# Attention on one core: scores, maxima and sums of the loop share eight PSUM banks by a build-time reckoning, half of the maxima 512 wide

## The chip, the core and the metric

The kernel runs on one core of a Trainium2 chip. The metric is device time in microseconds (us) from start to end of one execution. The core's engines run beside each other and wait for each other by semaphores: TensorE (PE in the profile; its weight loads are the row PEld), VectorE (DVE), ScalarE (ACT), GpSimd (POOL) and SyncE (SP), which here issues the DMAs. PE writes its results to PSUM, which has eight banks of 512 float32 values in each of 128 partitions; DVE and ACT read them there.

## What is computed

Two attention layers, A and B, are computed from inputs of 2048 rows of 640 columns, with 32 heads of 20 columns each. A looks back over 8 positions with a step of 2; B is full attention, and B is what the loop below does. The two results stand side by side in the output.

```python
# A: per head, 8 keys and values at distance 0, 2, .. 14
logits = jnp.where(mask, jnp.einsum("bhsd,bhswd->bhsw", q, kg) * Dh**-0.5, -1e9)
o_a = jnp.einsum("bhsw,bhswd->bhsd", softmax(logits), vg)   # then @ wo
# B: per head, all 2048 keys
scores = jnp.einsum("bhqd,bhkd->bhqk", q, k) * Dh**-0.5
o_b = jnp.einsum("bhqk,bhkd->bhqd", softmax(scores), v)     # then @ wo
```

## The kernel before

Before the loop PE projects A's and B's inputs to queries, keys and values. A's attention itself is done by POOL, in pieces that are handed out along the program; A's output projection is 32 pieces (`a_out`) of 15 matmuls of 320 columns each, and these pieces are worked into B's loop. They are called fills below.

B's loop (lines 794 to 838) runs over 512 steps. Heads are taken in 8 groups of 4, queries in 4 chunks of 512, keys in 16 blocks of 128: a step is one block of keys for one chunk of queries and one group. In step i:

- `b_qk` (644) makes the scores of four heads, keys in partitions and queries in columns: two planes (`pl`) of two matmuls (`r`). Each matmul uses 62 rows, and the two of a plane stand in the upper and the lower half of PE's rows, so that they run side by side. ACT takes the exponential of each into a tile e, 512 wide.
- `b_pv` (666) multiplies the exponentials of step i - 2 (LAG) with the values, in 8 PE passes; the row of ones among the values gives the sums. Two steps are added up in one bank, and ACT copies it out in every second step.
- `b_max` (618) finds the row maxima that step i + 24 (LEAD) will need. Scores are made once more, with queries in partitions, four matmuls of 512 columns; DVE takes the maximum of two banks in one instruction (1024 wide), twice a step. Maxima are turned, split and brought by DMA into the query tile (`max_rows`, 559), so that the score matmul itself subtracts them.

PSUM is shared in a fixed way: four single banks (`bank`, `give`, lines 87 to 99), used in turn by scores, sums and fills, and two double banks (`wide`, 101) for maxima. The order on every engine is the order in which the program calls the operations: `InOrder` (47) keeps it. In a step it is: first plane of scores, values of step i - 2, second plane of scores, first maximum, then perhaps a fill (every third pair of steps at most, lines 834 to 837), second maximum. Other work is due at a given step: `after(n, fn)` puts it n steps on, `tick` runs what is due, and `odd` moves some of it to steps of one parity.

In the last 24 steps no maxima are left; there scores use the double banks too. This tail (line 811) is followed by B's last output projection.

Of the kernel before, what the change touches and what calls it, by code (L numbers as in the profile page):

```python
# [2 lines left out]

# [5 lines left out]
F32 = mybir.dt.float32  # L9
F32R = mybir.dt.float32r  # L10
AF = mybir.ActivationFunctionType
ALU = mybir.AluOpType
# [20 lines left out]
BS = 3 * DH  # L33
# [13 lines left out]
class InOrder:  # L47


    def __init__(self, tc, engine):  # L50
        self.tc, self.engine = tc, engine

    def __getattr__(self, name):
        op = getattr(self.engine, name)
        return lambda *a, **k: self.tc.keep_in_program_order(op(*a, **k))  # L55


@with_exitstack
def attention_pair(ctx, tc, xa, wqk_a, wv_a, wo_a, xb, wqk_b, wv_b, wo_b, oa, ob):
# [3 lines left out]
    sb = ctx.enter_context(tc.tile_pool(name="sb", bufs=1))  # L63
    ps = ctx.enter_context(tc.tile_pool(name="ps", bufs=1, space=PS))
    dr = ctx.enter_context(tc.tile_pool(name="dr", bufs=1, space=bass.MemoryType.DRAM))
    pe, dve, act, gp, sp = (InOrder(tc, e) for e in (nc.tensor, nc.vector, nc.scalar, nc.gpsimd, nc.sync))


    now = [0]
# [14 lines left out]
            fn(*args)  # L84


    free = list(range(4))
    taken = {}

    def bank():  # L90

        n = free.pop(0)
        t = ps.tile([128, 512], F32, tag=f"st{n}", bufs=1, name="ps_st")
        taken[id(t)] = (n, t)
        return t

    def give(t):

        free.append(taken.pop(id(t))[0])

    def wide():

        return ps.tile([128, 2, 512], F32, tag="mx", bufs=2, name="ps_mx")

    def all_banks():
        while True:
# [452 lines left out]
    def max_rows(m4, m1, q, qc):  # L559

        mt = sb.tile([128, 3, 32], F32R, tag="mtr", bufs=2, name="mtr")
        md = dr.tile([2, GH * 512], F32, tag="mdr", bufs=4, name="mdr")
        raw = mt[:, 0].bitcast(F32)

        def turn():

            dve.transpose(raw, m1)

        def parts():
            gp.tensor_copy(mt[:, 1], raw)  # L570
            gp.tensor_tensor(mt[:, 2], raw, mt[:, 1].bitcast(F32), ALU.subtract)

        def store():
            for b in range(4):
                sp.dma_start(md.rearrange("t (j b c) -> b j t c", b=4, c=32)[b], mt[32 * b:32 * b + 16, 1:].bitcast(F32))

        def load():
            for r in range(2):
                sp.dma_start(q[r * HALF + BS:r * HALF + BM, qc].bitcast(F32),
                             md[:, r * 1024:(r + 1) * 1024].rearrange("t (p c) -> t p c", p=2))  # L580
        t = odd(1)
        after(t, dve.tensor_reduce, m1[:, :16], m4.rearrange("p r a c -> p (r a) c"), AX.X, ALU.max)
        after(t, turn)
        after(t + 1, parts)
        after(t + 3, store)
        after(t + 4, load)
# [28 lines left out]
    for t in m1s:  # L615
        gp.memset(t, 0.0)

    def b_max(i):

        u, sub = divmod(i, NKB)  # L620
        g, qc = divmod(u, NQC)
        q, k, v = stacks[g]
        if sub == 0:
            mxt[u] = (sb.tile([128, 2, 8, 4], F32, tag="mx4", bufs=2, name="mx4"),
                      m1s[u % 2])
        m4, m1 = mxt[u]
        pq, ch = divmod(sub, 2)
        pl, qb = divmod(pq, 4)
        for c in (2 * ch, 2 * ch + 1):
            p = wide()  # L630
            for r in range(2):
                rows = slice(r * HALF, r * HALF + BS)
                pe.matmul(p[:, r], q[rows, qc, pl, qb * 128:qb * 128 + 128],
                          k[rows, pl, c * 512:(c + 1) * 512], start=True, stop=True)
            dve.tensor_reduce(m4[:, :, pq, c], p, AX.X, ALU.max)
            if c % 2 == 0:
                yield
        if sub == NKB - 1:
            max_rows(m4, m1, q, qc)

    P = {}
    accs, raws, spare = {}, {}, []

    def b_qk(i):
        u, kb = divmod(i, NKB)
        g, qc = divmod(u, NQC)
        q, k, v = stacks[g]
        P[i] = []
        for pl in range(2):
            w = wide() if pl and i + LEAD >= NS else None  # L650
            ps2 = [bank() for _ in range(2)] if w is None else [w[:, 0], w[:, 1]]
            for r in range(2):
                rows = slice(r * HALF, r * HALF + BM)
                pe.matmul(ps2[r], k[rows, pl, kb * 128:kb * 128 + 128], q[rows, qc, pl], start=True, stop=True)
            if i + LEAD >= NS and i % 2:
                e = sb.tile([128, 2, 512], F32, tag="akv", bufs=4, name="e")
            else:
                e = sb.tile([128, 2, 512], F32, tag="p", bufs=PB, name="e")
            for r in range(2):
                act.activation(e[:, r], ps2[r], AF.Exp, scale=SCALE)  # L660
                if w is None:
                    give(ps2[r])
            P[i].append(e)
            yield

    def b_pv(i):
        u, kb = divmod(i, NKB)
        g, qc = divmod(u, NQC)
        n, part = divmod(kb, 2)
        if part == 0:  # L670
            accs[u] = bank()
        acc = accs[u]
        for j in range(GH):
            pe.matmul(acc[32 * j:32 * j + 32, :], stacks[g][2][:, kb, j * VC:j * VC + 32], P[i][j % 2][:, j // 2],
                      start=(part == 0), stop=(part == 1))
        del P[i]
        if part == 0:
            return
        if n == 0:
            raws[u] = sb.tile([128, 512], F32, tag="raw", bufs=2, name="braw")  # L680
            act.copy(raws[u], acc)
        else:
            more = spare[n % 2][:, n // 2 % 2]
            act.copy(more, acc)
            after(1, pool, raws[u], raws[u], more, ALU.add)
        give(accs.pop(u))
        if kb == NKB - 1:
            last = g == NG - 1
            normalize(raws.pop(u), g, qc * 512, 2 if last else 5, (lambda: out_last(qc)) if last else None)


    outs_b = {}
# [53 lines left out]
    for n, half, s in V_GROUPS[:-LAG]:  # L746
        v_group(n, half, s)
        tick()
        groups += 1
        if q_loads:  # L750
            for _ in range(4):
                q_loads.pop(0)()
        if groups == 1:
            wait[0] = 5
        if groups in (8, 16):
            XB[groups // 8 - 1], more = x_pieces(xb, groups // 8 - 1, gp)
            for fn in more:
                fn()
        if groups > 6:
            for i in islice(steps, 1):  # L760
                for _ in b_max(i):
                    pass
        if groups > 16 and groups % 3 == 0 and groups != 21:
            next(a_work, None)
        if groups in (26, 28):
            v_piece(0, *((0, 4) if groups == 26 else (8, 16)))
# [5 lines left out]
    def load_out(src, W, halves=range(2)):  # L772
        for h in halves:
            w, more = wide_pieces(src[h], gp)
            W.append(w)
            loads.extend(more)
# [14 lines left out]

    WO_b = []
    loop[0] = now[0] + 1
    for i in range(NS + LAG):
        g, sub = divmod(i, NQC * NKB)
        if sub == 4 and g + 1 < NG:
            k_loads, q_loads = b_pieces(g + 1)
            for n, fn in enumerate(k_loads + q_loads + [lambda g=g + 1: v_piece(g, 0, NKB)]):
                after(1 + 2 * n, fn)
        if i in (NS - 56, NS - 40):  # L800
            out_first((i - NS + 56) // NKB)
        tick()
        if loads and i % 2:
            loads.pop(0)()
        if i % 14 in (1, 5, 7, 11) and next(a_work, 0) == 0:
            for d in done_a:
                d[0] -= 1
        if done_a and done_a[0][0] <= 0:
            a_turn(*done_a.pop(0)[1:])
        turn_parts()  # L810
        if i + LEAD >= NS:

            for _ in b_qk(i) if i < NS else ():
                pass
            if i % 2:
                b_pv(i - LAG - 1)
                b_pv(i - LAG)
                if fill:
                    fill.pop(0)()
            continue  # L820
        qk = b_qk(i) if i < NS else iter(())
        next(qk, None)
        if i >= LAG:
            b_pv(i - LAG)
        else:
            v_group(*v_late.pop(0))
            if not v_late:
                load_out(wo_a, WO, (1,))

                spare += [sb.tile([128, 2, 512], F32, tag="last0", bufs=2, name="more") for _ in range(2)]  # L830
        next(qk, None)
        mx = b_max(i + LEAD)
        next(mx, None)
        if fill and i % 2 == 0:
            fill.pop(0)()
        elif i % 6 == 4 and not out_piece() and not left_a[0] and not WO_b:
            load_out(wo_b, WO_b)
        next(mx, None)


    qc = NQC - 1
# [54 lines left out]
```

## Time and profile before

| | us |
|---|---|
| median of 3 runs | 1843.13 |
| lowest and highest run | 1841.50 and 1843.66 |
| the profiled execution | 1841.84 |
| its span, first to last instruction | 1840.0 |
| PE busy in the span | 1796.4 |
| ACT busy | 1356.7 |
| DVE busy | 1318.5 |
| POOL busy | 1214.9 |

The granted clock of PE is 0.999 over the span. Names are those of the program's tiles: ps_st is a single bank, ps_mx a double one, e the exponentials, mx the maxima, bq and bk B's queries and keys, vb its values, ww and aot the output weights and A's turned result, more and braw the sums copied out. "out<-in" is what an instruction writes and reads. All instructions bear line L55, that of the helper that records them, so rows are told apart by engine and tiles. A row of the order of time has start, length, engine, operation and count, and in square brackets how long the engine stood idle before it and what ended that. A row of the waits has who waited for whom, the total in us, how often, and the longest.

### The profile page before, as it was taken

To read this page: it belongs to the slowest core of one execution; us is meant where nothing else is said; L and a number is where in the kernel's file an instruction comes from. 1 tells how busy PE (TensorE), PEld (TensorE's weight loads), DVE (VectorE), ACT (ScalarE), POOL (GpSimd) and SP (SyncE) were. 2 spreads that over 40 slices of the span, in tenths; PEclk is the share of its full clock that TensorE was granted. 3 is DMA by queue.
4 is the path that set the end of the run, shared out by engine and by line. 5 is a ranking of instruction groups with operands and counts; after the bars stand their busy time and mean duration, and the time that the engine had idled before them with its cause. 6 is when DMAs were issued, how large, how long until landed. Compare 5 with 4: busy or idle time off the path is not lost. (4 is left out here: it accounts for less than half of the span.)

```text
span 1840.0 us, 30597 instructions
## 1 busy us (share of the span) xinstructions
PE 1796.4 (98%) x11211; PEld 961.8 (52%) x11211; DVE 1318.5 (72%) x1350; ACT 1356.7 (74%) x2597; POOL 1214.9 (66%) x1072
## 2 busy tenths in 40 slices
PE   9999999999999999999999999999999999999999
PEld 8888888886344343343343333433434434433568
DVE  3100332278898989989989999899898898899400
ACT  4222322224898989989989999899898898899891
POOL 0000076028999999989999999999999872254232
PEclk9999999999999999999999999999999999999999
DMA  6323686656543544354435435344544331121023
GB/s 224 111 93 107 206 297 243 214 175 181 149 131 114 142 140 124 112 149 139 122 98 143 152 112 152 111 137 120 152 144 115 93 101 55 36 71 49 28 69 112
DMA packets 193006, 240.23 MB, mean 131 GB/s; under 512 B 90972, under 2 KB 121308, under 8 KB 191864
## 3 DMA queue, kind: packets, MB, share of 16 engines
q1 hardware_dynamic: 192280, 237.63, 42.4%
q8 instruction: 88, 1.44, 0.3%
q10 hardware_dynamic: 576, 0.66, 0.1%
q14 instruction: 62, 0.51, 0.1%
HBM read 173.29 MB, written 64.91 MB: 129 GB/s over the span
## 5 line engine op out<-in xcount | busy, mean ns | idle before, releaser
L55 DVE TENSOR_REDUCE mx<-ps_mx 128x2 f32<-128x1024 f32 x1024 | 1198.3, 1217 | 133.8 <-PE ps_mx L55 131.9
L55 ACT ACTIVATE e<-ps_st 128x512 f32<-128x512 f32 x2000 | 1063.4, 608 | 50.3 <-PE ps_st L55 22.2
L55 PE MATMUL ps_st<-e,vb 128*32 128x512 f32 x4096 | 543.6, 605 | 0.6
L55 PE MATMUL ps_st<-bq,bk 62*128 62x512 f32 x2000 | 471.0, 455 | 2.0 <-DMA bq<-mdr 2.0
L55 PEld LDWEIGHTS ps_st<-bq,bk 62*128 62x128 f32 x2000 | 249.4, 184 | 424.4 <-ACT e L55 408.2
L55 PE MATMUL ps_mx<-bk,bq 60*128 60x512 f32 x2048 | 421.0, 442 | 34.9 <-DVE mx L55 16.7
L55 POOL TENSOR_TENSOR braw<-braw,more 128x512 f32<-128x512 f32 x224 | 287.7, 1284 | 178.5 <-ACT more L55 170.4
L55 POOL TENSOR_TENSOR akv<-akv,aq 128x1280 f32<-128x1280 f32 x64 | 188.9, 2952 | 237.4 <-DMA akv<-ka_d 237.4
L55 PEld LDWEIGHTS ps_mx<-bk,bq 60*128 60x128 f32 x2048 | 192.1, 185 | 203.5 <-DVE mx L55 193.5
L55 POOL TENSOR_TENSOR akv<-akv 128x640 f32<-128x640 f32 (+3 forms) x304 | 281.4, 926 | 23.8
L55 PEld LDWEIGHTS ps_st<-e,vb 128*32 128x32 f32 x4096 | 82.0, 108 | 157.2 <-ACT e L55 82.0
L55 ACT COPY ro<-ps_st 128x320 f32<-128x320 f32 (+1 forms) x92 | 43.6, 474 | 154.7 <-PE ps_st L55 110.1
L55 POOL TENSOR_TENSOR akv<-akv,al 128x1280 f32<-128x1280 f32 x64 | 151.5, 2367 | 0.2
L55 ACT COPY more<-ps_st 128x512 f32<-128x512 f32 x224 | 132.8, 593 | 12.9 <-PE ps_st L55 2.8
L55 PE MATMUL ps_st<-ww,xn 128*128 128x320 f32 x720 | 120.1, 315 | 0.0
L55 PEld LDWEIGHTS ps_st<-ww,xn 128*128 128x128 f32 x720 | 106.6, 188 | 20.9 <-ACT e L55 9.1
L55 POOL TENSOR_TENSOR xn<-stg,xn 128x512 fp32r<-128x512 f32 (+1 forms) x20 | 30.1, 1508 | 94.8 <-ACT xn L55 93.5
L55 DVE TENSOR_TENSOR wc<-stg,wc 128x480 fp32r<-128x480 f32 (+5 forms) x15 | 8.4, 559 | 101.5 <-ACT wc L55 101.5
L55 PE MATMUL ps_st<-ww,aot 128*128 128x320 f32 x480 | 79.0, 316 | 0.0
L55 POOL TENSOR_TENSOR ao<-ao,akv 128x640 f32<-128x640 f32 x48 | 74.9, 1560 | 3.8
L55 DVE TENSOR_TENSOR xl<-stg,xl 128x512 fp32r<-128x512 f32 x12 | 8.3, 689 | 96.2 <-ACT xl L55 96.2
L55 PEld LDWEIGHTS ps_st<-ww,aot 128*128 128x128 f32 x480 | 70.5, 188 | 11.7 <-ACT e L55 5.8
(84 smaller groups left out, 1312.2 us busy)
## 6 DMA issues: line engine op xcount, KB each, us to landing
akv<-ka_d SPq DMA_DIRECT2D x128, 320.0 KB
akv<-va_d SPq DMA_DIRECT2D x128, 320.0 KB
kb_d<-pr SPq DMA_DIRECT2D x20, 512.0 KB
qb_d<-pr SPq DMA_DIRECT2D x20, 512.0 KB
bk<-kb_d SPq DMA_DIRECT2D x16, 640.0 KB
bq<-qb_d SPq DMA_DIRECT2D x64, 160.0 KB
rb<-s_d SPq DMA_DIRECT2D x128, 64.0 KB
stg<-xb SPq DMA_DIRECT2D x12, 512.0 KB
```

The costliest lines, as they stand in the source:

```text
L55: return lambda *a, **k: self.tc.keep_in_program_order(op(*a, **k))
```

## The change

All of PSUM becomes one tile of eight banks, psb. Before the loop and in its tail, banks are given out as before: 0 to 3 singly, 4 to 7 in two doubles.

In the steps with maxima the loop goes by pairs of steps (`b_pair`). The 8 score matmuls and 8 maximum matmuls of a pair are put in eight brackets of two (`b_two`), one matmul in each half of PE's rows. Four brackets hold a score and one matmul of a maximum; two hold both matmuls of a maximum, two hold two scores. A maximum whose matmuls share a bracket is reduced 1024 wide from two banks in a row, the others 512 wide, one bank each: per pair two wide and four narrow instead of four wide.

Which bank each matmul writes is chosen while the program is built. `InOrder` adds up a time for ACT and DVE with each operation, `b_pv` and `b_two` do so for PE, and `read_at` holds for each bank when its last reader should be done. `one` picks the bank that is ready first, `two` the two neighbours. The program that results is fixed; the waits in it still follow the real data. A fill takes a bank by the same reckoning, and is issued in odd steps, behind the fifth bracket of a pair (its second `yield`). Work that is due at odd steps now falls behind the third bracket. The diff's core:

```diff
+        def emit(*a, **k):
+            self.us += self.fixed + max([math.prod(x.shape[1:]) for x in a if hasattr(x, "shape")], default=0) / self.rate
+            return self.tc.keep_in_program_order(op(*a, **k))
...
+    dve, act = InOrder(tc, nc.vector, 0.075, 960), InOrder(tc, nc.scalar, 0.111, 1400)
...
+    psb = ps.tile([128, 8, 512], F32, name="ps_st")
...
     def bank():
 
+        if read_at:
+            n = one(pe.us)
+            pe.us = max(pe.us, read_at[n]) + 2.2
+            act.us = max(act.us, pe.us + 0.05)
+        else:
+            n = free.pop(0)
+        t = psb[:, n]
...
+    def one(t, *but):
+
+        at = [1e9] + read_at + [1e9]
+        return min((n for n in range(8) if n not in but), key=lambda n: (
+            max(t, read_at[n]), -max(t, at[n]) - max(t, at[n + 2])))
+
+    def two(t):
+
+        return min(range(7), key=lambda n: (max(t, read_at[n], read_at[n + 1]), abs(read_at[n] - read_at[n + 1])))
...
     def b_pv(i):
...
+        if read_at:
+            t = max(pe.us + 0.12, exp_at.pop(i))
+            if part == 0:
+                o = one(t)
+                accs[u] = o, psb[:, o]
+                t = max(t, read_at[o])
+                read_at[o] = 1e9
+            pe.us = t + 0.866
+            behind_v[0] = True
...
+    def b_two(what):
+
+        t = pe.us + 0.129 * behind_v[0]
+        lag = 0.53 if behind_v[0] else 0.44
+        both = what[0][0] == what[1][0] == "m"
+        if both:
+            n = two(t)
+            ns, ts = (n, n + 1), [max(t, read_at[n], read_at[n + 1])] * 2
+        else:
+            ns, ts = [], []
+            for _ in range(2):
+                ns.append(one(max([t] + ts), *ns))
+                ts.append(max([t] + ts + [read_at[ns[-1]]]))
+        pe.us = ts[1] + (0.236 if ts[1] > ts[0] + 0.05 or (ts[0] < t + 0.02 and not behind_v[0]) else 0.336)
+        behind_v[0] = False
+        for (kind, *at), n in zip(what, ns):
+            (s_matmul if kind == "s" else m_matmul)(*at, psb[:, n])
+        for (kind, i, j, r), n, t in zip(what, ns, ts):
+            if kind == "s":
+                act.us = max(act.us, t + lag)
+                s_exp(i, j, r, psb[:, n])
+                exp_at[i] = act.us + 0.2
+                read_at[n] = act.us + 0.18
+            elif not both or r == 1:
...
+                if both:
+                    dve.tensor_reduce(m4[:, :, pq, 2 * ch + j], psb[:, ns[0]:ns[0] + 2], AX.X, ALU.max)
+                    read_at[ns[0]] = dve.us + 0.13
+                else:
+                    dve.tensor_reduce(m4[:, r, pq, 2 * ch + j:2 * ch + j + 1], psb[:, n], AX.X, ALU.max)
+                read_at[n] = dve.us + 0.13
+
+    def b_pair(i, pv):
+
+        m = i + LEAD
+        max_tiles(m)
+        s = [("s", i + j, pl, r) for j in range(2) for pl in range(2) for r in range(2)]
+        pv(i - LAG)
+        b_two([s[0], ("m", m, 0, 1)])
+        b_two([("m", m, 1, 0), ("m", m, 1, 1)])
+        b_two([s[1], s[2]])
+        yield
+        pv(i - LAG + 1)
+        b_two([s[3], ("m", m, 0, 0)])
+        b_two([("m", m + 1, 0, 0), ("m", m + 1, 0, 1)])
+        yield
+        b_two([s[4], s[5]])
+        b_two([s[6], ("m", m + 1, 1, 1)])
+        b_two([s[7], ("m", m + 1, 1, 0)])
+        max_end(m + 1)
...
+        if i % 2 == 0:
+            steps = b_pair(i, b_pv if i else lambda _: v_group(*v_late.pop(0)))
+        next(steps)
+        if i % 2 == 0:
+            continue
...
+        if fill:
             fill.pop(0)()
-        elif i % 6 == 4 and not out_piece() and not left_a[0] and not WO_b:
+        elif i % 6 == 5 and not out_piece() and not left_a[0] and not WO_b:
             load_out(wo_b, WO_b)
-        next(mx, None)
+        next(steps, None)
```

More of the change, by code (lines that the diff above doesn't have):

```diff
@@ L1 @@
+import math
 from contextlib import ExitStack
@@ L47, with __init__ @@
 class InOrder:
-    def __init__(self, tc, engine):
-        self.tc, self.engine = tc, engine
+    def __init__(self, tc, engine, fixed=0.0, rate=math.inf):
+        self.tc, self.engine, self.fixed, self.rate = tc, engine, fixed, rate
+        self.us = 0.0
     def __getattr__(self, name):
         op = getattr(self.engine, name)
-        return lambda *a, **k: self.tc.keep_in_program_order(op(*a, **k))
+        def emit(*a, **k):
+            self.us += self.fixed + max([math.prod(x.shape[1:]) for x in a if hasattr(x, "shape")], default=0) / self.rate
+            return self.tc.keep_in_program_order(op(*a, **k))
+        return emit
 @with_exitstack
@@ L65, in attention_pair @@
     dr = ctx.enter_context(tc.tile_pool(name="dr", bufs=1, space=bass.MemoryType.DRAM))
-    pe, dve, act, gp, sp = (InOrder(tc, e) for e in (nc.tensor, nc.vector, nc.scalar, nc.gpsimd, nc.sync))
+    pe, gp, sp = (InOrder(tc, e) for e in (nc.tensor, nc.gpsimd, nc.sync))
+    dve, act = InOrder(tc, nc.vector, 0.075, 960), InOrder(tc, nc.scalar, 0.111, 1400)
     now = [0]
@@ L84, in tick @@
             fn(*args)
+    psb = ps.tile([128, 8, 512], F32, name="ps_st")
     free = list(range(4))
+    pair = [0]
     taken = {}
+    read_at = []
     def bank():
-        n = free.pop(0)
-        t = ps.tile([128, 512], F32, tag=f"st{n}", bufs=1, name="ps_st")
+        if read_at:
[5 more added lines that the diff above has]
+        t = psb[:, n]
         taken[id(t)] = (n, t)
@@ L97, in give @@
     def give(t):
-        free.append(taken.pop(id(t))[0])
-    def wide():
-        return ps.tile([128, 2, 512], F32, tag="mx", bufs=2, name="ps_mx")
+        n = taken.pop(id(t))[0]
+        if read_at:
+            read_at[n] = act.us + 0.2
+        else:
+            free.append(n)
+    def wide():
+        pair[0] += 1
+        return psb[:, 4 + 2 * (pair[0] % 2):6 + 2 * (pair[0] % 2)]
+    def one(t, *but):
[4 more added lines that the diff above has]
+        return min(range(7), key=lambda n: (max(t, read_at[n], read_at[n + 1]), abs(read_at[n] - read_at[n + 1])))
     def all_banks():
@@ L616, in attention_pair, with max_tiles, m_matmul @@
         gp.memset(t, 0.0)
-    def b_max(i):
+    def max_tiles(i):
+        u, sub = divmod(i, NKB)
+        if sub == 0:
+            mxt[u] = (sb.tile([128, 2, 8, 4], F32, tag="mx4", bufs=2, name="mx4"),
+                      m1s[u % 2])
+        return mxt[u]
+    def m_matmul(i, j, r, p):
         u, sub = divmod(i, NKB)
@@ L622, in b_max, with max_end, s_matmul @@
         q, k, v = stacks[g]
[L623 to L629, printed above, removed]
+        pl, qb = divmod(sub // 2, 4)
+        c = sub % 2 * 2 + j
+        rows = slice(r * HALF, r * HALF + BS)
+        pe.matmul(p, q[rows, qc, pl, qb * 128:qb * 128 + 128], k[rows, pl, c * 512:(c + 1) * 512], start=True, stop=True)
+    def max_end(i):
+        u, sub = divmod(i, NKB)
+        if sub == NKB - 1:
+            max_rows(*mxt[u], stacks[u // NQC][0], u % NQC)
+    def b_max(i):
+        m4 = max_tiles(i)[0]
+        pq, ch = divmod(i % NKB, 2)
+        for j in range(2):
             p = wide()
             for r in range(2):
[L632 to L639, printed above, removed]
+                m_matmul(i, j, r, p[:, r])
+            dve.tensor_reduce(m4[:, :, pq, 2 * ch + j], p, AX.X, ALU.max)
+        max_end(i)
     P = {}
     accs, raws, spare = {}, {}, []
-    def b_qk(i):
+    def s_matmul(i, pl, r, p):
         u, kb = divmod(i, NKB)
@@ L647, in b_qk, with s_exp @@
         q, k, v = stacks[g]
-        P[i] = []
+        rows = slice(r * HALF, r * HALF + BM)
+        pe.matmul(p, k[rows, pl, kb * 128:kb * 128 + 128], q[rows, qc, pl], start=True, stop=True)
+    def s_exp(i, pl, r, p):
+        if i not in P:
+            P[i] = [None, None]
+        if P[i][pl] is None:
+            if i + LEAD >= NS and i % 2:
+                P[i][pl] = sb.tile([128, 2, 512], F32, tag="akv", bufs=4, name="e")
+            else:
+                P[i][pl] = sb.tile([128, 2, 512], F32, tag="p", bufs=PB, name="e")
+        act.activation(P[i][pl][:, r], p, AF.Exp, scale=SCALE)
+    def b_qk(i):
         for pl in range(2):
-            w = wide() if pl and i + LEAD >= NS else None
+            w = wide() if pl else None
             ps2 = [bank() for _ in range(2)] if w is None else [w[:, 0], w[:, 1]]
             for r in range(2):
[L653 to L658, printed above, removed]
+                s_matmul(i, pl, r, ps2[r])
             for r in range(2):
-                act.activation(e[:, r], ps2[r], AF.Exp, scale=SCALE)
+                s_exp(i, pl, r, ps2[r])
                 if w is None:
                     give(ps2[r])
-            P[i].append(e)
-            yield
+    exp_at = {}
+    behind_v = [False]
     def b_pv(i):
@@ L669, in b_pv @@
         n, part = divmod(kb, 2)
-        if part == 0:
-            accs[u] = bank()
-        acc = accs[u]
+        if read_at:
+            t = max(pe.us + 0.12, exp_at.pop(i))
[6 more added lines that the diff above has]
+            behind_v[0] = True
+        elif part == 0:
+            accs[u] = None, bank()
+        o, acc = accs[u]
         for j in range(GH):
@@ L678, in b_pv @@
             return
+        del accs[u]
+        act.us = max(act.us, pe.us + 0.322)
         if n == 0:
@@ L685, in b_pv @@
             after(1, pool, raws[u], raws[u], more, ALU.add)
-        give(accs.pop(u))
+        if o is None:
+            give(acc)
+        else:
+            read_at[o] = act.us + 0.25
         if kb == NKB - 1:
@@ L689, in b_pv @@
             normalize(raws.pop(u), g, qc * 512, 2 if last else 5, (lambda: out_last(qc)) if last else None)
+    def b_two(what):
[5 more added lines that the diff above has]
+            ns, ts = (n, n + 1), [max(t, read_at[n], read_at[n + 1])] * 2
+        else:
+            ns, ts = [], []
[13 more added lines that the diff above has]
+            elif not both or r == 1:
+                pq, ch = divmod(i % NKB, 2)
+                m4 = mxt[i // NKB][0]
+                dve.us = max(dve.us, t + lag)
+                if both:
+                    dve.tensor_reduce(m4[:, :, pq, 2 * ch + j], psb[:, ns[0]:ns[0] + 2], AX.X, ALU.max)
+                    read_at[ns[0]] = dve.us + 0.13
+                else:
+                    dve.tensor_reduce(m4[:, r, pq, 2 * ch + j:2 * ch + j + 1], psb[:, n], AX.X, ALU.max)
[17 more added lines that the diff above has]
+        max_end(m + 1)
     outs_b = {}
@@ L760, in attention_pair @@
             for i in islice(steps, 1):
-                for _ in b_max(i):
-                    pass
+                b_max(i)
         if groups > 16 and groups % 3 == 0 and groups != 21:
@@ L793, in attention_pair @@
     loop[0] = now[0] + 1
+    read_at += 8 * [0.0]
+    for e in (pe, act, dve):
+        e.us = 0.0
     for i in range(NS + LAG):
@@ L811, in attention_pair @@
         if i + LEAD >= NS:
-            for _ in b_qk(i) if i < NS else ():
-                pass
+            read_at.clear()
+            if i < NS:
+                b_qk(i)
             if i % 2:
@@ L820, in attention_pair @@
             continue
[L821 to L832, printed above, removed]
-        next(mx, None)
-        if fill and i % 2 == 0:
+        if i % 2 == 0:
[3 more added lines that the diff above has]
+            continue
+        if i == 1:
+            load_out(wo_a, WO, (1,))
+            spare += [sb.tile([128, 2, 512], F32, tag="last0", bufs=2, name="more") for _ in range(2)]
+        if fill:
             fill.pop(0)()
-        elif i % 6 == 4 and not out_piece() and not left_a[0] and not WO_b:
+        elif i % 6 == 5 and not out_piece() and not left_a[0] and not WO_b:
             load_out(wo_b, WO_b)
-        next(mx, None)
+        next(steps, None)
     qc = NQC - 1
```

## The prediction

> **What bounds the kernel now.** I read the stretches first, then the groups of VectorE (DVE) in the loop, then the order of time. The stretch 441 to 1716 us is the loop of 488 steps (244 pairs) that carries the maxima; columns are length, then busy time and count of each engine.
>
> ```profile
> 441.00:1716.00 1275.00, 1238.64 (x8254) 503.49 (x8253) 1168.12 (x1170) 1160.38 (x2230) 1076.67 (x940) 1.00 0.40 118
> 1716.00:1840.00 124.00, 119.31 (x830) 87.05 (x828) 13.97 (x20) 75.77 (x155) 37.23 (x35) 1.00 0.24 78
> ```
>
> The loop is 1275 of the span's 1840.0 us. TensorE (PE), DVE (1168.12) and ScalarE (ACT, 1160.38) are each over 90% busy: no engine alone is the bound. The groups of DVE in that stretch (busy, mean ns | idle before):
>
> ```profile
> L55 DVE TENSOR_REDUCE mx<-ps_mx 128x2 f32<-128x1024 f32 x971 | 1135.7, 1217 | 106.0 <-PE ps_mx L55 104.1
> L55 DVE STREAM_TRANSPOSE turn<-ao 128x128 f32<-128x128 f32 x80 | 23.7, 296 | 0.0
> ```
>
> DVE stands idle 106.0 us, nearly all of it for PE. Next, PE in an undisturbed stretch: two steps, from one score pair to the next but one.
>
> ```profile
> 1620.22 0.50 PE L55 MATMUL ps_st<-bq,bk 62*128 62x512 f32 x2
> 1620.56 1.01 PE L55 MATMUL ps_mx<-bk,bq 60*128 60x512 f32 x4
> 1621.41 0.49 PE L55 MATMUL ps_st<-bq,bk 62*128 62x512 f32 x2
> 1621.84 1.07 PE L55 MATMUL ps_st<-e,vb 128*32 128x512 f32 x8
> 1622.83 0.50 PE L55 MATMUL ps_st<-bq,bk 62*128 62x512 f32 x2
> 1623.17 0.75 PE L55 MATMUL ps_mx<-bk,bq 60*128 60x512 f32 x4
> 1623.76 0.41 PE L55 MATMUL ps_st<-bq,bk 62*128 62x512 f32 x2
> 1624.17 1.06 PE L55 MATMUL ps_st<-e,vb 128*32 128x512 f32 x8
> 1625.16 0.50 PE L55 MATMUL ps_st<-bq,bk 62*128 62x512 f32 x2
> ```
>
> A pair of steps takes 1625.16 - 1620.22 = 4.94 us. PE is called busy throughout, but its weight loads show what it waited for, here and over the whole run:
>
> ```profile
> 1621.08 0.19 PEld L55 LDWEIGHTS ps_mx<-bk,bq 60*128 60x128 f32 x2 [0.56 <-DVE mx L55]
> 1623.41 0.18 PEld L55 LDWEIGHTS ps_mx<-bk,bq 60*128 60x128 f32 x2 [0.28 <-DVE mx L55]
> ...
> PEld ps_st L55 <- ACT e L55: 505.1, 770, 1.6
> PEld ps_mx L55 <- DVE mx L55: 195.3, 442, 1.0
> ```
>
> The reader is to see a ring: PE waits for banks that ACT (four banks) and DVE (two double banks) have not read, and both then wait for PE. The ring, not an engine, sets 4.94 us.
>
> **The change part by part.** *Cost on DVE.* Of four 1024-wide maxima in a pair, two become four 512-wide ones: 488 more instructions (in the built program DVE's count rises from 1352 to 1840). No 512-wide maximum is in this trace. Two maxima with no wait between them show the spacing, and four with small waits a little more; a 512-wide and a 1024-wide subtraction show what width costs, and a 512-wide one that reads PSUM is the nearest row:
>
> ```profile
> 1589.23 2.36 DVE L55 TENSOR_REDUCE mx<-ps_mx 128x2 f32<-128x1024 f32 x2
> 1633.49 4.68 DVE L55 TENSOR_REDUCE mx<-ps_mx 128x2 f32<-128x1024 f32 x4 [0.25 <-PE ps_mx L55]
> ...
> L55 DVE TENSOR_TENSOR xn<-stg,xn 128x1024 fp32r<-128x1024 f32 x14 | 17.2, 1225 | 34.3 <-ACT xn L55 34.3
> L55 DVE TENSOR_TENSOR pr<-ps_mx,pr 128x512 fp32r<-128x512 f32 x20 | 13.8, 692 | 48.7 <-ACT pr L55 48.7
> ```
>
> Spacing 2.36 - 1.217 = 1.143 us; width 1.225 - 0.692 = 0.533 us per 512 columns; so a start costs 1.143 - 2 x 0.533 = 0.077 us of DVE where instructions follow each other, and 0.692 - 0.533 = 0.159 us where nothing overlaps. The ends for the added instructions are 488 x 0.077 = 38 us and 488 x 0.159 = 78 us; I take 38, since the added maxima stand in line as those of the row do.
>
> The Trainium skill (VectorE: DVE Perf Modes, "The TRN2 errata") gives an instruction that reads PSUM 120 cycles plus its width at 0.96 GHz, an estimate of 0.125 us per start: the 488 would cost 61 us. The row of 1.143 us, where that rule gives 1.192, speaks for less.
>
> *DVE's floor.* 976 wide maxima's worth at 1.143 us is 1116 us; the rest of DVE's work adds, overlap taken off, 1168.1 - 1135.7 = 32 us; the added starts 38 us: 1186 us, or 4.86 us a pair.
>
> *What the banks give back.* The changed kernel issues in a pair: values (pv), [score, max half], [wide max], [two scores], pv, [score, max half], [wide max], [two scores], [score, max half], [score, max half]; each bracket is two matmuls side by side. The build shows the banks: the third score pair's first matmul takes one that the first wide maximum leaves; the next pv takes that of the score just before. The prices: bracket to bracket 0.34 us where it waits (1623.17 - 1622.83), 0.24 where not (1623.41 - 1623.17); bracket to pv 0.41; pv to bracket 0.99. The end of a reader to PE, and ACT's pace, come from these:
>
> ```profile
> 1619.81 3.55 DVE L55 TENSOR_REDUCE mx<-ps_mx 128x2 f32<-128x1024 f32 x3
> ...
> 1642.76 0.59 ACT L55 COPY more<-ps_st 128x512 f32<-128x512 f32 x1
> 1647.69 0.59 ACT L55 COPY more<-ps_st 128x512 f32<-128x512 f32 x1
> 1652.69 0.59 ACT L55 COPY more<-ps_st 128x512 f32<-128x512 f32 x1
> 1653.18 2.08 ACT L55 ACTIVATE e<-ps_st 128x512 f32<-128x512 f32 x4
> ```
>
> The first maximum ends at 1619.81 + 1.217 = 1621.03, and PE's load follows at 1621.08: 0.05 us. Exponentials (0.60 us each) are (2.08 - 0.60)/3 = 0.49 us apart. From a matmul to its reader it is 0.44 us (1596.77 to 1597.21, in the next fence) to 0.55 us. Then: brackets at 0, 0.34, 0.58; pv 0.99; brackets 1.98, 2.32; the first wide maximum runs 1.30 to 2.52, so the two scores start at 2.58; ACT has a copy from 2.17, exponentials from 2.66 and 3.15, whose bank is free at 3.80; there the next pv starts, and the pair ends at 3.80 + 0.99 = 4.79 us. DVE's own part, 2 x 1.143 + 4 x 0.61 = 4.73 us, nearly fills that; ACT's, 9 x 0.49 = 4.41, does not; PE's without waits is 2 x (0.99 + 0.41) + 2 x 0.34 + 4 x 0.24 = 4.44. So DVE is late next: its idle outside the fills falls to about 8 us in all, 0.06 a pair of which its other work eats most.
>
> *The fills.* Thirty-two times 15 output matmuls stand in the loop (480 of them). In the old order:
>
> ```profile
> 1591.06 0.50 PE L55 MATMUL ps_st<-bq,bk 62*128 62x512 f32 x2
> 1593.71 0.39 PE L55 MATMUL ps_mx<-bk,bq 60*128 60x512 f32 x2
> 1594.03 2.46 PE L55 MATMUL ps_st<-ww,aot 128*128 128x320 f32 x15
> 1596.43 0.51 PE L55 MATMUL ps_mx<-bk,bq 60*128 60x512 f32 x2
> 1596.77 0.40 PE L55 MATMUL ps_st<-bq,bk 62*128 62x512 f32 x2
> 1598.10 0.50 PE L55 MATMUL ps_st<-bq,bk 62*128 62x512 f32 x2
> ...
> 1596.98 1.23 DVE L55 TENSOR_REDUCE mx<-ps_mx 128x2 f32<-128x1024 f32 x1 [1.61 <-PE ps_mx L55]
> 1598.88 1.23 DVE L55 TENSOR_REDUCE mx<-ps_mx 128x2 f32<-128x1024 f32 x1 [0.67 <-PE ps_mx L55]
> ...
> 1597.21 1.09 ACT L55 ACTIVATE e<-ps_st 128x512 f32<-128x512 f32 x2 [0.25 <-PE ps_st L55]
> ```
>
> That pair takes 1598.10 - 1591.06 = 7.04 us, 2.10 more; DVE is idle 1.61 + 0.67 - 0.25 (its usual gap) = 2.03 us. The fill moves behind the second wide maximum. There PE stands 2.2 us; DVE has that maximum left, until 4.25 on the scale above, and gets the next at 5.6, then runs 0.6 short until a backlog is back: 1.9 us idle. Eight banks can't hold a fill's worth of work ahead, so I take 32 x 1.9 = 61 us.
>
> *At nothing.* Work before the loop and the tail (124 us) keep their instructions; each engine's but DVE's are the same in number, DMAs too. Fills and some loads move by one step: POOL, at 1077 of 1275 us, covers a late one; bare, each would cost up to the step, 2.5 us, and a handful move. ACT gets 650 more separate wait instructions; in the rows above 1652.69 + 0.49 is the next start, so they are issued beside running work. Bound 0 to 0.08 us each, 0.2 us a pair, which ACT's 4.86 - 4.41 covers; without that cover 52 us. One tile for all banks costs nothing: the build waits bank by bank.
>
> *Sum.* 1186 + 8 + 61 = 1255 against 1275: 20 us less. The profiled execution took 1841.84 us, so 1821.8; the median of the runs lies 1.3 us above that execution, which I add but for rounding: **1822 us**.
>
> **The rivals.** *The added starts are not overlapped (slower).* Each narrow maximum costs 0.159 us beyond its width: 41 us more, 1863 us. It decides from (38 + 20)/488 = 0.119 us a start. For it: only one undisturbed spacing, of wide ones; against: four in line at (4.68 - 1.217)/3 = 1.154 us, and the added ones stand in fuller queues. The page's rule above is this rival at 0.125 us: slightly slower than before.
>
> *The waits only move.* Banks are fixed at build time by reckoned ends; where the engines run otherwise, PE waits for a bank that is late while another is free. If half of DVE's idle time outside the fills (106.0 - 32 x 2.03 = 41 us) and of the spacing lost at gaps (1136 - 1110 = 26 us) stays, about 33 us come back less the 8 counted: 25 us, 1847 us; if all, 1880. The change then doesn't do what it says. For it: PE's, ACT's and DVE's clocks are all reckoned, and DMAs are not; against: the ring's prices are regular, as the copies above follow each other after 1647.69 - 1642.76 = 4.93 and 1652.69 - 1647.69 = 5.00 us.
>
> *The fills are swallowed.* If PE, with 0.35 us a pair to spare, fills the banks ahead and half of each fill hides, 32 x 1.0 = 32 us go, and 8 us of idle: 1784 us. Against: the 8 banks are full in my schedule at 3.3 to 3.8.
>
> **How the numbers follow.** Forecast, 1805 to 1837: 0.46. Added starts dear, 1850 to 1866: 0.17. Waits move, 1838 to 1880: 0.21, half of it within 0.2%. Fills swallowed, 1780 to 1805: 0.16. About 0.2% (3.7 us) is what a measurement can tell from no change. Faster 0.46 + 0.16 = 0.62; same 0.11; slower 0.17 + 0.10 = 0.27. The range 1790 to 1868 leaves out some 0.1 at each end; the likeliest case's own is 1805 to 1837.
>
> **What would show it.** Undisturbed pairs at 4.8 to 4.9 us; 512-wide maxima 0.61 us apart; DVE idle in the loop near 70 us, in lumps at the fills; pairs with a fill 1.8 to 2.0 us longer; PE's waits for ACT far below 505 us. I am wrong if narrow maxima are 0.66 us or more apart, if undisturbed pairs stay at 4.94, or if a fill costs under 1.5 us.

## The result, and the profile after

The changed kernel takes 1812.83 us (median of 4 runs, 1812.22 to 1817.24) against 1842.32 us (4 runs); the ratio is 0.9847, with a 95% interval of 0.9827 to 0.9868. So it is 29.5 us faster; 20 us were forecast (1822 us). The profiled execution is the slowest of the four, 1817.24 us; beside the 1841.84 us of before that is 24.6 us, and this is what the two traces can explain.

The loop is compared over the same 244 pairs of steps in both. They end a little later than the stretch that the prediction took: 440 to 1728 us before, 444 to 1707 us after. Of the kernel before, the stretch and DVE's maxima in it:

```profile
440.00:1728.00 1288.00, 1251.21 (x8336) 510.77 (x8332) 1176.72 (x1177) 1169.59 (x2248) 1079.32 (x943) 1.00 0.40 117
...
L55 DVE TENSOR_REDUCE mx<-ps_mx 128x2 f32<-128x1024 f32 x977 | 1142.9, 1217 | 110.4 <-PE ps_mx L55 108.5
```

Of the kernel after, the same (columns as before):

```profile
444.00:1707.00 1263.00, 1256.76 (x8340) 546.58 (x8340) 1191.53 (x1666) 1140.58 (x2248) 1077.98 (x941) 1.00 0.41 119
...
L60 DVE TENSOR_REDUCE mx<-ps_st 128x1 f32<-128x512 f32 x976 | 630.0, 681 | 68.8 <-PE ps_st L60 66.1
L60 DVE TENSOR_REDUCE mx<-ps_st 128x2 f32<-128x1024 f32 x488 | 594.1, 1217 | 0.0
```

The loop is 25 us shorter. DVE is busy 1191.5 - 1176.7 = 14.8 us longer, and idle for 1263.0 - 1191.5 = 71.5 us where it was 1288.0 - 1176.7 = 111.3, 39.8 us less: the difference is the gain. Nearly all of the idle time is spent waiting for PE, ahead of maxima (110.4 and 68.8 us). Two steps of the changed kernel in an undisturbed stretch, PE first, then the weight loads that waited for a bank with no values' matmuls running before them, then DVE:

```profile
1600.13 0.49 PE L60 MATMUL ps_st<-bq,bk 62*128 62x512 f32 x1
1600.13 0.77 PE L60 MATMUL ps_st<-bk,bq 60*128 60x512 f32 x3
1600.71 0.70 PE L60 MATMUL ps_st<-bq,bk 62*128 62x512 f32 x3
1601.02 0.43 PE L60 MATMUL ps_st<-bk,bq 60*128 60x512 f32 x1
1601.44 0.50 PE L60 MATMUL ps_st<-bq,bk 62*128 62x512 f32 x1
1601.46 0.50 PE L60 MATMUL ps_st<-bk,bq 60*128 60x512 f32 x1
1601.95 1.06 PE L60 MATMUL ps_st<-e,vb 128*32 128x512 f32 x8
1602.95 0.50 PE L60 MATMUL ps_st<-bq,bk 62*128 62x512 f32 x1
1602.95 0.73 PE L60 MATMUL ps_st<-bk,bq 60*128 60x512 f32 x3
1603.53 0.40 PE L60 MATMUL ps_st<-bq,bk 62*128 62x512 f32 x2
1603.86 1.07 PE L60 MATMUL ps_st<-e,vb 128*32 128x512 f32 x8
1604.85 0.49 PE L60 MATMUL ps_st<-bq,bk 62*128 62x512 f32 x1
...
1601.44 0.18 PEld L60 LDWEIGHTS ps_st<-bq,bk 62*128 62x128 f32 x1 [0.30 <-DVE mx L60]
1601.95 0.16 PEld L60 LDWEIGHTS ps_st<-e,vb 128*32 128x32 f32 x8 [0.31 <-ACT e L60]
...
1598.81 7.30 DVE L60 TENSOR_REDUCE mx<-ps_st 128x1 f32<-128x512 f32 x9 [0.15 <-PE ps_st L60]
```

(The nine of DVE's row are wide and narrow mixed; the row shows the first one's shape.) The pair takes 1604.85 - 1600.13 = 4.72 us, where it was 4.94. PE still waits, but DVE's row marks no wait inside the pair (a row of several instructions does not mark waits under 0.15 us). PE's waits for ACT's banks in the loop fell, those for DVE's did not; before, then after:

```profile
PEld ps_st L55 <- ACT e L55: 492.7, 749, 1.6
PEld ps_mx L55 <- DVE mx L55: 189.0, 417, 0.9
```

```profile
PEld ps_st L60 <- ACT e L60: 374.6, 693, 1.0
PEld ps_st L60 <- DVE mx L60: 187.9, 340, 2.7
```

A pair with a fill, after (PE at the pair's start, at the fill and at the next pair, then DVE):

```profile
1571.65 0.50 PE L60 MATMUL ps_st<-bq,bk 62*128 62x512 f32 x1
1574.31 2.47 PE L60 MATMUL ps_st<-ww,aot 128*128 128x320 f32 x15
1576.71 0.72 PE L60 MATMUL ps_st<-bq,bk 62*128 62x512 f32 x3
1578.61 0.49 PE L60 MATMUL ps_st<-bq,bk 62*128 62x512 f32 x1
...
1577.50 1.29 DVE L60 TENSOR_REDUCE mx<-ps_st 128x1 f32<-128x512 f32 x2 [1.56 <-PE ps_st L60]
1579.17 6.65 DVE L60 TENSOR_REDUCE mx<-ps_st 128x1 f32<-128x512 f32 x8 [0.38 <-PE ps_st L60]
```

It takes 6.96 us, and DVE is idle 1.56 + 0.38 = 1.94 us. Counted over all 32 fills in the trace, DVE's idle time in the 5.5 us from a fill's first matmul is 1.75 us on average, 56 of its 71.5 idle us (before: 2.13 us, 68 of 111.3). Outside the fills its idle time falls from 43 to 15 us: there DVE is now nearly the bound.

Counted over the loop by the start of every eighth exponential, without the first two pairs and the last few, pairs without a fill take 4.87 us on average (4.98 before) and pairs with one 6.95 (7.06 before). The averages lie above the undisturbed pair; that some pairs also hold DVE's other work fits this, but was not traced pair by pair.

### The profile page after: what moved, and what is told of

The parts are those of the page before. It is cut to its first block, busy times and chain, and to the rows that moved or that the text cites. A ratio compares the mean times of both kernels' runs of the same rounds, so it can differ in the third digit from the quotient of the medians.

```text
span 1815.5 us, 31747 instructions
## 1 busy us (share of the span) xinstructions
PE 1802.0 (99%) x11211; PEld 997.7 (55%) x11211; DVE 1333.1 (73%) x1838; ACT 1326.9 (73%) x2597; POOL 1214.9 (67%) x1072
## 5 line engine op out<-in xcount | busy, mean ns | idle before, releaser
L60 DVE TENSOR_REDUCE mx<-ps_st 128x1 f32<-128x512 f32 (+1 forms) x1512 | 1214.9, 871 | 95.8 <-PE ps_st L60 93.1
L60 PE MATMUL ps_st<-bq,bk 62*128 62x512 f32 x2048 | 632.6, 445 | 2.7 <-DMA bq<-mdr 1.8
L60 PE MATMUL ps_st<-bk,bq 60*128 60x512 f32 x2048 | 592.3, 442 | 4.3 <-DMA bq<-qb_d 1.7
L60 PEld LDWEIGHTS ps_st<-bq,bk 62*128 62x128 f32 x2048 | 285.1, 184 | 526.2 <-ACT e L60 315.8
L60 PEld LDWEIGHTS ps_st<-bk,bq 60*128 60x128 f32 x2048 | 274.3, 184 | 44.8 <-DVE mx L60 17.4
L60 ACT COPY ro<-ps_st 128x480 f32<-128x480 f32 (+1 forms) x124 | 61.2, 495 | 238.0 <-PE ps_st L60 183.5
L60 PE MATMUL ps_st<-wc,xn 128*128 128x480 f32 x576 | 135.7, 380 | 0.6 <-ACT xn L60 0.6
L60 PEld LDWEIGHTS ps_st<-wc,xn 128*128 128x128 f32 x576 | 107.9, 188 | 18.3 <-ACT xn L60 1.2
L60 PE MATMUL ps_st<-xn,w 128*128 128x512 f32 x480 | 115.8, 390 | 0.0
L60 PEld LDWEIGHTS ps_st<-xn,w 128*128 128x128 f32 x480 | 90.1, 188 | 19.3
```

The lines of the kernel that those rows point to most:

```text
L60: return self.tc.keep_in_program_order(op(*a, **k))
```

## The experiments

All medians stand against the changed kernel's 1812.83 us; "pair" is the average of pairs without a fill, counted as above, and pv is the values' matmuls (`b_pv`). Every ratio is to the kernel before, measured beside the run. Three theories were set against each other. Ring: banks that both readers may use are what frees the pair. Halves: 512-wide maxima give banks back sooner. Order: a score beside half a maximum feeds ACT and DVE evenly.

**Old order, shared banks.**

```diff
-        pv(i - LAG)
-        b_two([s[0], ("m", m, 0, 1)])
...
+        w = [[("m", m + j, c, 0), ("m", m + j, c, 1)] for j in range(2) for c in range(2)]
+        b_two([s[0], s[1]])
+        pv(i - LAG)
+        b_two([s[2], s[3]])
+        b_two(w[0])
+        b_two(w[1])
+        yield
+        b_two([s[4], s[5]])
+        pv(i - LAG + 1)
+        b_two([s[6], s[7]])
+        b_two(w[2])
+        yield
+        b_two(w[3])
```

> The order of the kernel before (two scores, values, two scores, two wide maxima, twice; a fill between the last two maxima), but banks shared by the reckoning. Ring theory: most of the 30 us stays, 1813 to 1825 us. Order theory and halves theory: none of it, 1838 to 1846 us.

Measured: 1854.4 us, ratio 1.0062 (1.0047 to 1.0077), pair 5.01 us. The ring theory in its bare form falls: sharing alone gives nothing. The trace shows the same undisturbed pair as before the change and why (the weight load of a second wide maximum, and DVE):

```profile
1702.24 0.19 PEld L60 LDWEIGHTS ps_st<-bk,bq 60*128 60x128 f32 x2 [0.63 <-DVE mx L60]
...
1704.70 2.36 DVE L60 TENSOR_REDUCE mx<-ps_st 128x2 f32<-128x1024 f32 x2 [0.24 <-PE ps_st L60]
```

Of two wide maxima in a row the second needs two banks that an earlier maximum holds; PE stands before it, and later DVE stands for PE, 0.24 us, as before the change (0.25).

**Old order, shared banks, every other maximum in halves.** As above, and

```diff
-        both = what[0][0] == what[1][0] == "m"
+        both = what[0][0] == what[1][0] == "m" and what[0][2] == 1
```

> Old order of brackets, banks shared by the reckoning, and every other maximum as two 512-wide ones, so DVE has the changed kernel's instructions. Halves theory (sharing and narrow maxima together are enough): 1813 to 1830 us. Order theory (the brackets that hold a score and half a maximum are needed as well): as the old order with shared banks and wide maxima, which took 1854 us, or up to 23 us above it for the added starts.

Measured: 1860.2 us, ratio 1.0098 (1.0083 to 1.0113), pair 5.04. Halves with sharing are not enough either, with the banks chosen at these prices: the order is needed as well.

**New order and halves, fixed banks.**

```diff
-    def one(t, *but):
+    def one(t, *but, of=range(4)):
...
-        return min((n for n in range(8) if n not in but), key=lambda n: (
+        return min((n for n in of if n not in but), key=lambda n: (
...
-        return min(range(7), key=lambda n: (max(t, read_at[n], read_at[n + 1]), abs(read_at[n] - read_at[n + 1])))
+        return min(range(4, 7), key=lambda n: (max(t, read_at[n], read_at[n + 1]), abs(read_at[n] - read_at[n + 1])))
...
+            for kind, *_ in what:
+                ns.append(one(max([t] + ts), *ns, of=range(4) if kind == "s" else range(4, 8)))
```

> The changed kernel's order and its narrow maxima, but banks 0 to 3 are kept for scores, sums and fills, and 4 to 7 for maxima; the reckoning chooses within each four. Ring theory: PE waits for ACT's banks as before, pairs at 4.9 or more, 1840 to 1860 us. Order and halves theories: the sharing adds nothing, 1813 to 1820 us.

Measured: 1851.5 us, ratio 1.0044 (1.0029 to 1.0058), pair 4.95; PE's waits for ACT's banks are 597.3 us over the run, where the changed kernel has 388.2. With the new order, sharing is worth 39 us; with the old one it was worth less than nothing. Neither works without the other.

**All wide.** Each maximum gets a bracket of its own and scores go in twos: pv, [s0 s1], [wide], [s2 s3], pv, [s4 s5], [wide], [wide], [s6 s7], [wide].

> The changed kernel with all four maxima of a pair 1024 wide, each in a bracket of its own, and scores in brackets of two; banks are still shared by the reckoning. Ring theory (banks that both readers may use are what frees the pair of steps): DVE has 488 starts less, 4 x 1.13 = 4.52 us a pair, so at most 0.05 us a pair above the changed kernel's 4.71, 1813 to 1825 us. Halves theory (512-wide maxima give banks back sooner, and that is what frees it): undisturbed pairs near 4.94 again, about 1842 us. Order theory (a score beside a maximum feeds ACT and DVE evenly): near 1842 us too.

Measured: 2018.3 us, ratio 1.0949 (1.0932 to 1.0965), pair 5.78. None of the theories allowed that. The order differs in more than the widths (one maximum ahead of one pv, three ahead of the other), so the run alone settles nothing; the runs on the last two brackets below were made for that.

**All narrow.**

```diff
-        both = what[0][0] == what[1][0] == "m"
+        both = False
```

> The changed kernel with all eight maximum matmuls of a pair reduced 512 wide: 488 more maxima again. If DVE bounds the loop, they cost a start each: 0.05 us (two narrow at 0.585 us in the changed kernel's trace against one wide at 1.13) gives 20 to 25 us more, 1835 to 1838 us; the 0.077 us of the prediction gives 38 us, 1850 us. If the bank wait bounds it and halves free banks sooner, 1813 us or less.

Measured: 1835.5 us, ratio 0.9957 (0.994 to 0.9974): 22.7 us more for 488 more starts, 0.047 us each. The expectation's lower price of a start, 0.05 us, held; the prediction's 0.077 us, which meant 1850 us, did not. DVE runs 38 narrow maxima in a row here, and the second line is fifteen of them, seen through a narrower window:

```profile
1641.85 23.24 DVE L60 TENSOR_REDUCE mx<-ps_st 128x1 f32<-128x512 f32 x38
1642.42 9.05 DVE L60 TENSOR_REDUCE mx<-ps_st 128x1 f32<-128x512 f32 x15
```

The 38 are (23.24 - 0.68)/37 = 0.610 us apart on average, but three waits of under 0.1 us lie among them, which the row does not mark. The fifteen have none, and are (9.05 - 0.68)/14 = 0.598 us apart. Two narrow maxima in the place of a wide one, 1.143 us, so cost DVE 2 x 0.598 - 1.143 = 0.053 us, near the 0.047 that the run paid. The Trainium skill's rule (VectorE: DVE Perf Modes, "The TRN2 errata") makes an estimate of 0.658 us of a narrow one's spacing; the trace is below it.

**One maximum merged.** The halves in the last two brackets stay there, in neighbouring banks, and are reduced once.

```diff
-        b_two([s[6], ("m", m + 1, 1, 1)])
-        b_two([s[7], ("m", m + 1, 1, 0)])
+        b_merged(m + 1, s[6], s[7])
```

(`b_merged` takes neighbours by `two`, keeps both until the second matmul, and reduces 1024 wide.)

> The changed kernel, same order of matmuls and shared banks, but the maximum whose halves stand in the last two brackets of a pair is reduced once, 1024 wide, from two neighbouring banks, when its second half is there: 244 starts of DVE less, and one bank held a bracket longer. If DVE's starts are what bounds the loop: 244 x 0.047 = 11 us less, 1802 us. If the early return of single banks is what gave the gain (halves theory): 1820 us or more.

Measured: 1873.1 us, ratio 1.0165 (1.015 to 1.0181), pair 5.12. Fewer starts, and 60 us more.

**The last two brackets apart: narrow, wide, and wide first.** Three kernels with one difference from each to the next: scores and maximum matmuls in separate brackets, still narrow; the same, reduced 1024 wide; the same, with the maximum ahead.

```diff
-        b_two([s[6], ("m", m + 1, 1, 1)])
-        b_two([s[7], ("m", m + 1, 1, 0)])
+        b_two([s[6], s[7]])
+        b_two([("m", m + 1, 1, 0), ("m", m + 1, 1, 1)])
```

> The changed kernel, but its last two brackets (score and half a maximum, twice) become one of two scores and one of two halves, still reduced 512 wide. If a bracket must feed both readers (mixing), 1825 us or more; if the single banks and the count of maxima before each pv are what matters, 1810 to 1820 us.

> As the run before, with that last maximum reduced once, 1024 wide: 244 starts of DVE less. DVE as the bound: 10 to 15 us under the run before. Single banks as what matters: 15 us or more above it, as the merged maximum cost 60 us.

> As the run before with the two brackets changed over: the wide maximum, then the two scores. DVE's work arrives one bracket sooner ahead of pv, ACT's one later. If DVE is late at pv, some 5 to 15 us less than the run before; if ACT is, as much more.

Measured: narrow 1817.8 us (ratio 0.9864, 0.9848 to 0.988), not told apart from the changed kernel; wide 1969.2 us (1.0684, 1.0668 to 1.07); wide first 1859.4 us (1.0087, 1.0072 to 1.0102). So a bracket needn't feed both readers here, against the order theory's mixing. But one maximum in four, made whole, costs 151 us, though it takes 244 starts off DVE. In the wide kernel's trace the two weight loads of that maximum stand one after the other (PE's loads, then DVE):

```profile
1624.12 0.18 PEld L60 LDWEIGHTS ps_st<-bk,bq 60*128 60x128 f32 x1 [0.32 <-DVE mx L60]
1625.10 0.18 PEld L60 LDWEIGHTS ps_st<-bk,bq 60*128 60x128 f32 x1 [0.79 <-ACT e L60]
...
1625.63 1.23 DVE L60 TENSOR_REDUCE mx<-ps_st 128x2 f32<-128x1024 f32 x1 [0.43 <-PE ps_st L60]
```

A wide maximum needs two neighbours at once. The first is free at 1624.12, the second only at 1625.10, when ACT has read a score out of it. PE works in order, so the second matmul starts 0.98 us behind the first, although the two could run side by side, and DVE starts at 1625.63, 0.43 us idle. Two halves may take any two banks. A wide maximum also gives both of its banks back only at its end; how much of the 151 us is that, and how much the neighbours, was not measured apart. With the wide maximum ahead of the last scores some 110 of the 151 us go, where 5 to 15 were expected; PE's waits for ACT's banks over the run are 454.5 us there and 587.5 with the scores first.

**Rotation.** No reckoned times: a counter takes their place, so that the bank read longest ago in program order is taken.

```diff
-                read_at[n] = dve.us + 0.13
+                read_at[n] = turn()
```

(and so for each such line, and in `one` and `two`, without the other terms of their keys.)

> The changed kernel, but no reckoned times: a bank is taken by whichever was last read longest ago in program order, a double one by its later half. If sharing and order do the work, 1813 to 1822 us; if the reckoned times do, 1835 us or more, since PE then waits for a bank of the slower engine while another is free.

Measured: 1945.4 us, ratio 1.0557 (1.054 to 1.0575), pair 5.45. Of PE's waits over the run, those for DVE's banks are now the largest:

```profile
PEld ps_st L60 <- DVE mx L60: 455.2, 669, 1.0
PEld ps_st L60 <- issue: 323.6, 629, 0.8
```

PE waits in turn for a bank that DVE still holds.

**A wrong reckoning.**

```diff
-    dve, act = InOrder(tc, nc.vector, 0.075, 960), InOrder(tc, nc.scalar, 0.111, 1400)
+    dve, act = InOrder(tc, nc.vector, 0.150, 960), InOrder(tc, nc.scalar, 0.111, 1400)
```

> The changed kernel with DVE's fixed part in the reckoning set to 0.150 us, where 0.064 to 0.075 is real; only the choice of banks can change. If the choice needs true times, 1830 us or more, towards the 1945 us of the rotation; if any choice that knows which engine reads a bank will do, 1811 to 1820 us.

Measured: 1869.3 us, ratio 1.014 (1.0125 to 1.0155), pair 5.11. The same instructions in the same order on every engine, other banks: 57 us. A mistake of 0.075 us in one price of the plan turns the gain into a loss.

**Fills in thirds.** Each fill goes out as 5 + 5 + 5 matmuls in three pairs that follow each other.

```diff
-                rows15(p, lambda xi, k: ot[:, xi, k], W[half])
+                for part in range(3):
+                    if part:
+                        yield
...
+                    for m in range(5 * part, 5 * part + 5):
+                        k, (wi, xi) = m // 3, PASSES[m % 3]
+                        pe.matmul(p[:, :320], ot[:, xi, k], W[half][wi][:, k], start=m == 0, stop=m == 14)
...
-        elif i % 6 == 5 and not out_piece() and not left_a[0] and not WO_b:
+        elif not out_piece() and not left_a[0] and not WO_b:
```

> The changed kernel with every fill of 15 matmuls in the loop given out as three lots of 5 in three pairs that follow each other; it holds one bank all that time. PE has 4.71 - 4.44 = 0.27 us to spare a pair by the prediction's prices, and 96 lots of 0.67 us and two changes of mode take its place. If a fill costs DVE's idle time alone: 3 x (0.27 + 0.05) = 1 us of each fill's 2.2 is covered, 20 to 30 us less, 1785 to 1795 us. If the held bank or the changes of mode cost as much: 1813 us or more.

Measured: 1844.1 us, ratio 1.0008 (0.9999 to 1.0017). A pair with a third takes 5.84 us on average, about 0.97 more than one without, so a fill costs 2.9 us where it cost 2.1. PE at a third:

```profile
563.82 1.05 PE L60 MATMUL ps_st<-bk,bq 60*128 60x512 f32 x3
564.80 1.00 PE L60 MATMUL ps_st<-ww,aot 128*128 128x320 f32 x5
565.74 0.73 PE L60 MATMUL ps_st<-bq,bk 62*128 62x512 f32 x3
```

The five matmuls keep PE from its brackets for 565.74 - 564.80 = 0.94 us, where a third of a whole fill's 1576.71 - 1574.31 = 2.40 us is 0.80; the pair grows by as much, so nothing of it is hidden, against the 1 us of each fill that was to be covered. How much the bank that it holds for three pairs adds was not measured by itself.

None of these beats the changed kernel; the narrow one with the last brackets apart is level with it.

## Why the prediction was right, point by point

- *DVE's floor.* Forecast: 1186 us for the 976 maxima and the rest. DVE is busy 1191.5 us, so the level was right within 6 us. Two terms behind it were not, and they cancel, which is luck. The added starts were put at 488 x 0.077 = 38 us; by the spacing of narrow maxima without waits they are 488 x 0.053 = 26 us. The price was worked out from wide maxima, and narrow ones come cheaper. And the overlap of one maximum with the next, which is lost at each wait (26 us before), was to come back whole; 1191.5 - (1116 + 32 + 26) = 17 us of it is still lost.
- *DVE's idle time.* Forecast: 106 us falls to 8 + 61 = 69 us. It is 68.8 us ahead of the maxima and 71.5 in all: some 15 outside the fills and 56 at them. That PE's waits go to where they no longer starve DVE was the heart of the forecast, and it held; the undisturbed pair is 4.72 us, forecast 4.79 with DVE's own 4.73 close behind. With narrow maxima 0.598 us apart DVE's own part is 2 x 1.143 + 4 x 0.598 = 4.68 us.
- *The fills.* Forecast: 1.9 us of DVE's idle time each; measured 1.94 in the fill shown and 1.75 on average. They stay the largest piece of DVE's idle time, as forecast. A pair with a fill is still 6.95 - 4.87 = 2.08 us longer than one without, as it was before (7.06 - 4.98), where 1.8 to 2.0 was the forecast.
- *The sum.* 20 us forecast, 24.6 between the profiled executions, 29.5 between medians. That the forecast comes so near is luck in part. The changed loop was forecast at 1255 us and takes 1263. It was set beside 1275 us, where the loop ended 12 us before the last of the 244 pairs; beside the true 1288 the same terms would have promised 33 us, and 25 came. One error hid the other. The 5 us between 24.6 and 29.5 lie between the changed kernel's profiled execution and its other three runs, of which there is no trace. One thing fits: 0.997 of the full clock was granted in the profiled one, 0.999 to 1.0 in the others. That the clock is the cause is not shown.
- *At nothing.* POOL is busy 1079.3 us in the loop before and 1078.0 after; DVE's transposes take 23.7 us in both. ACT's added wait instructions cost nothing that shows where ACT has work: five exponentials took 2.56 us at 1600.81, (2.56 - 0.60)/4 = 0.49 us apart, as before. Outside the loop the profiled executions differ by 4 us ahead of it and 3 us behind it, the other way round; no cause was looked for.
- *The rivals.* Dear starts: refuted by 0.598 us, or 0.610 with waits. Fills swallowed: refuted by 1.75 us, where 1.0 was the rival's. The waits that only move: it did not come about in this kernel, but I gave it too little room as a mechanism: some 17 us of lost overlap and 15 of idle time outside the fills are what is left of those waits. Rotation, a wrong price, and fixed banks each let it decide, at 1945, 1869 and 1851 us. What speaks for the changed kernel is not eight shared banks, as my ring had it, but this order with these halves and this choice of banks.

Of the cause, this is shown: the gain needs sharing (fixed banks, 39 us), true prices in the reckoning (57 us; without any, 133 us), and singles in place of a wide maximum (151 us at one place, in the variant with the last brackets apart). Open stays whether the old order could gain with a reckoning made for it: in the runs with the old order the banks were chosen with the same prices and the same rule as in the changed kernel, and with merged maxima nearly so; I did not try others. A choice of banks alone moves the time by 57 us and more, so the runs that change order or widths show what these do under this reckoning, not under the best one for each.

The Trainium skill has two rules that bear on this. Perfetto Trace Analysis, "Matmul Optimizations", asks to use all eight banks; both kernels do, and the one that shared them in the old order was slower (1854 us). The Trainium skill, on the same page (Perfetto Trace Analysis, "Optimizing Scalar/DVE Operations"), says that breaking up instructions may help where an engine is not saturated but makes others wait, and that larger operations help where it is saturated. The runs agree with both halves in the new order: one more maximum broken up gained 151 us (1969 to 1818), all four broken up cost 22.7 us, DVE being near its bound by then. In the old order, breaking up two of four gained nothing (1854 and 1860 us).

## What to carry to other kernels

Where an in-order engine writes banks for two readers, look for the wait in which it stands for one reader while the other runs dry; a smaller piece that fits any single free bank can be worth more than the instruction start that it costs. A plan of banks fixed at build time is only as good as its prices: take them from the trace, and test the plan with one of them wrong. Forecast by the busy and idle time of the engine that is late next, over exactly the same steps in both kernels, and price an added instruction from a row of its own width where one can be had.

## What the runs showed that I had not expected

- How steep the ground around the changed kernel is: with all its arithmetic the same, other banks alone made 1869 and 1945 us, and one of four maxima reduced whole made 1969 us.
- Each visit of PE to a fill has a price of its own: 5 matmuls of a fill take 0.94 us of PE, 15 take 2.40 us, so about 0.2 us go with each visit ((3 x 0.94 - 2.40)/2 = 0.21). That it is PE's change from matmuls side by side to full ones and back is likely, but was not tested.
